# A weight load cut in two column halves, and the order of two steps' side work, in a fused attention and GELU kernel

## The chip, the cores and the metric

The kernel runs on one core of one Trainium2 chip. The metric is the time of the program on the device in microseconds (us): the median of 3 runs is 198.84 us (198.81 to 199.01).

## What is computed

A linear attention with decay, for 4 batches, 8 heads, 768 positions and 64 channels per head, and then a feed-forward pair of matrix products with a GELU (tanh form) between them. Cut to what matters:

```python
for b in range(nb):                       # blocks of 64 positions
    intra = einsum('bhic,bhjc->bhij', qb, kb) * Dmask     # scores, masked and decayed
    intra = einsum('bhij,bhjd->bhid', intra, vb)
    inter = einsum('bhid,bhde->bhie', qb * lam_pow, kv_state)
    out[:, :, sl] = intra + inter
    kv_state = lam_block * kv_state + einsum('bhsd,bhse->bhde', kb * rev_pow, vb)
x = out.transpose(0, 2, 1, 3).reshape(3072, 512)
h = x @ w_in                              # 512 x 2048
g = 0.5 * h * (1 + tanh(c * (h + 0.044715 * h ** 3)))
return g @ w_out                          # 2048 x 512
```

Inputs and the output are float32; the matrix products run on float16 copies.

## The kernel before

**Steps.** The attention is worked in 24 steps. A step is 256 positions of four of the eight heads (`half`) of one batch; two steps make a block of 256 rows of x. A step `s` passes through these pieces, each a small function:

- `load_step` issues three DMAs (q, k, v, 256 KB each, in rows of 512 bytes) on the queue of SyncE (SP).
- `prep` scales q by its decay and casts it (L282, VectorE, called DVE in the profile), casts k (L295, ScalarE, called ACT; at step 4 L293 on DVE), and scales v (L266, GpSimd, called POOL).
- `stage_t` transposes q and k for steps 0 to 7: eight 128x128 matmuls against the identity (L321, TensorE, called PE) into the PSUM tile Tps, and one copy to the tile qkT (L328 on ACT for steps 5 and 6, L330 on DVE for steps 4 and 7; steps 0 to 3 share it between the two). From step 8 on a transposing DMA does it (L303).
- `scores(n)` makes the scores S from qkT: 16 matmuls on 64x64 tiles (L350).
- `products(n, s)` makes step n's update of the state, K (L385), and step s's outputs, from the masked scores PT and v (L399) and from the state u and q (L408), all in two PSUM tiles named OK. With `evacuate` it ends with `x_out(s)`: ACT copies OK to xT, the x of the feed-forward part (two copies, L487).
- `causal(n)` multiplies S by the mask into PT: two operations on DVE (L360).
- `update(n, c, parts)` carries the state on: part "t" on DVE (L506, or L503 at a batch's start), part "u" on POOL (L513).

`R(n, s)` is a helper that calls `scores(n)`, `products(n, s)`, `causal(n)` and `update(n, 0)` in that order; `U(n)` is `update(n, 1)`. At step 5, the last of its batch in its half, `U` issues nothing.

**Weights.** `load_win(j, part)` loads the quarter j of w_in (512 of its 2048 columns, L94); the first two quarters come in two parts of 512 KB each (`part` chooses half of the 512 rows). `cast_win` makes the float16 copies: the second part of the first quarter is cast by ACT for columns 0 to 255 (two operations of 128 columns, L108) and by DVE for columns 256 to 511 (one operation, L110). The matmuls of the feed-forward part's first product read them (L838 for the first group of rows, L561 after that). SP's queue has, in this order: q, k, v of steps 0 to 2, q and k of step 3, the first part of quarter 0, v of step 3, the second part of quarter 0, the rest of w_in, w_out, and q, k, v of steps 4 to 8. A DMA is issued when its tile is free.

**Order.** `pin` keeps every instruction in the order in which it is written, on its engine. So the order is written out by hand, at the function's end. The feed-forward work (product one: Hps, then GELU; product two: O2ps, four matmuls to a piece, L576; later groups MX, MY and MW, L640, in which sums of weights, made on DVE at L133, stand in for some of the products) is kept in the list `filler`, and `fill(n)` issues the next n pieces of it between the attention's steps: this is what TensorE does while other engines prepare the next step. [...]

Around the change the order is: `products(3, None)`, `causal(3)`, the casts of the second part of quarter 0 (ACT and DVE), `update(3, 0)`, `fill(4)` (the first four pieces to read these casts), `products(None, 3)`; and, later, `R(5, 4)`, `stage_t(6)`, `U(5)`, `prep(7)`, a sum of weights on DVE, `fill(2)`, `R(6, 5)`, `U(6)`, `fill(1)`, `prep(8)`.

Of the kernel before, what the change touches and what calls it, by code (L numbers as in the profile page):

```python
# [15 lines left out]
def kernel(  # L16
# [10 lines left out]
    nc = tc.nc  # L27
    pin = tc.keep_in_program_order
# [59 lines left out]
    def load_win(j, part=None):  # L88
        if not part:
            wstage[("i", j)] = wst.tile([P, NC, 512], FP32, tag=f"w{j}", name=f"wi32_{j}")  # L90
        t = wstage[("i", j)]
        src = moe_w_in[:, j * 512 : (j + 1) * 512].rearrange("(c p) f -> p c f", p=P)
        cs = slice(0, NC) if part is None else slice(2 * part, 2 * part + 2)
        pin(nc.sync.dma_start(out=t[:, cs, :], in_=src[:, cs, :]))  # L94

    def load_wout(j):
        t = wst.tile([P, 4, DM], FP32, tag=f"w{(0, 2, 1, 3)[j]}", name=f"wo32_{j}")
# [147 lines left out]
    def prep(s):  # L245
        prep_qk(s)
        prep_v(s)
# [61 lines left out]
    def stage_t(s):  # L309
        if s >= FIRST_DMA_T:  # L310
            return
        tq, tk = a16[s][:2]
        if s < 4:
            Tps = [ps_M.tile([P, 2, 2, P], FP16, tag="M", name=f"Tps{i}") for i in range(2)]
        else:
            Tps = ps_M.tile([P, 2, 2, 2, P], FP16, tag="M", name="Tps")
        for i, t in enumerate((tq, tk)):
            to = Tps[i] if s < 4 else Tps[:, i]
            for hp in range(2):
                for j in range(2):  # L320
                    pin(nc.tensor.transpose(to[:, j, hp, :], t[:, j, 2 * hp : 2 * hp + 2, :],  # L321
                                            ident[:]))
        o = qkp.tile([P, 2, 2, 2, P], FP16, tag="qkT", name=f"qkT_{s}")
        if s < 4:
            pin(nc.scalar.activation(out=o[:, 0], in_=Tps[0][:], func=AF.Copy))
            pin(nc.vector.tensor_copy(out=o[:, 1], in_=Tps[1][:]))
        elif s in (5, 6, 8):
            pin(nc.scalar.activation(out=o[:], in_=Tps[:], func=AF.Copy))  # L328
        else:
            pin(nc.vector.tensor_copy(out=o[:], in_=Tps[:]))  # L330
        qkT[s] = o
# [7 lines left out]
    def half64(i):  # L339
        return slice(64 * i, 64 * i + 64)  # L340
# [3 lines left out]
    def scores(n):  # L344
        o = qkT[n]
        Sps = [ps_M.tile([P, 2, 2, P], FP32, tag="M", name=f"S{hl}") for hl in range(2)]
        for hp in range(2):
            for jk in range(2):
                for hl, c in TILES:
                    pin(nc.tensor.matmul(  # L350
                        Sps[hl][half64(c), hp, jk, :], o[half64(hl), 1, jk, hp, half64(c)],
                        o[half64(hl), 0, :, hp, half64(c)], start=True, stop=True,
                        skip_group_check=True))
        Ss[n] = Sps

    def causal(n):

        t = ptp.tile([P, 2, 2, 2, P], FP16, tag="PT", name=f"PT_{n}")
        for hl, Sps in enumerate(Ss.pop(n)):
            pin(nc.vector.tensor_tensor(  # L360
                t[:, hl].rearrange("p b c d -> p b (c d)"), Sps[:].rearrange("p b c d -> p b (c d)"),
                mask[:].unsqueeze(1).to_broadcast([P, 2, 2 * P]), ALU.mult))
        PTs[n] = t

    def products(n, s, banks=None, evacuate=True):


        OK, opened = banks or ([ps_M.tile([P, 512], FP32, tag="M", name=f"OK{c}")
                                for c in range(2)], set())

        def start(c, hl):
            if (c, hl) in opened:
                return False
            opened.add((c, hl))
            return True

        if n is not None:
            _, tk, tv = a16[n]
            last = (n // 2) % NSB == NSB - 1
            for jk in range(2):  # L380
                for hp in range(2):
                    for c, hl in TILES:
                        if c == 1 and last:
                            continue
                        pin(nc.tensor.matmul(  # L385
                            OK[c][half64(hl), 256 + hp * D : 256 + hp * D + D],
                            tk[half64(c), jk, 2 * hp + hl, :], tv[half64(c), jk, 2 * hp + hl, :],
                            start=start(c, hl), stop=(jk == 1), skip_group_check=True))
            Kps[n] = [t[:, 256:384] for t in OK]
        if s is None:  # L390
            return OK, opened
        sbg, half = divmod(s, 2)
        o = qkT.pop(s)
        PT = PTs.pop(s)
        _, _, tv = a16.pop(s)
        for hp in range(2):
            for jk in range(2):
                for c, hl in TILES:
                    pin(nc.tensor.matmul(  # L399
                        OK[c][half64(hl), hp * P : hp * P + P], tv[half64(c), jk, 2 * hp + hl, :],  # L400
                        PT[half64(c), hl, hp, jk, :], start=start(c, hl), stop=False,
                        skip_group_check=True))
        for c in range(2):
            if c == 0 and sbg % NSB == 0:
                continue
            u = us.pop((s, 0) if c else (s - 2, 1))
            for hp in range(2):
                pin(nc.tensor.matmul(OK[c][:, hp * P : hp * P + P], u[:, hp].rearrange("p l d -> p (l d)"),  # L408
                                     o[:, 0, :, hp, half64(c)], start=False, stop=True,
                                     skip_group_check=True))  # L410
        if evacuate:
            x_out(s, OK)
        return OK, opened
# [61 lines left out]
    def x_out(s, OK, second=None):  # L475
        sbg, half = divmod(s, 2)
        g, i = group_of[sbg]
        if g not in xT:
            xT[g] = xtp.tile([P, 2, len(groups[g]), 2, SB], FP16, tag="xT", name=f"xT_{g}")
        dst = xT[g][:, half, i]  # L480
        for c in range(2):
            d = dst[:, :, c * P : (c + 1) * P].rearrange("p hp (t j) -> p hp j t", j=2)
            o = OK[c][:, 0:256].rearrange("p (hp j t) -> p hp j t", hp=2, j=2)
            if c == 1 and second is not None:
                pin(second.tensor_copy(out=d, in_=o))
            else:
                pin(nc.scalar.activation(out=d, in_=o, func=AF.Copy))  # L487
# [3 lines left out]
    def update(s, c, parts="tu"):  # L491


        sbg, half = divmod(s, 2)
        sb = sbg % NSB
        if c == 1 and sb == NSB - 1:
            Kps.pop(s)
            return
        if "t" in parts:
            K = (Kps[s] if c == 0 else Kps.pop(s))[c].rearrange("p (hp d) -> p hp d", hp=2)  # L500
            t = ucp.tile([P, 2, D], FP32, tag=f"t{half}", name=f"t_{s}_{c}")
            if sb == 0 and c == 0:
                pin(nc.vector.tensor_copy(out=t[:], in_=K))  # L503
            else:
                for hp in range(2):
                    pin(nc.vector.scalar_tensor_tensor(  # L506
                        t[:, hp, :], state[half][:, hp, :],
                        lamu[:, 2 * half + hp : 2 * half + hp + 1], K[:, hp, :],
                        ALU.mult, ALU.add))
            state[half] = t  # L510
        if "u" in parts:
            u = ubp.tile([P, 2, 2, D], FP16, tag=f"u{half}", name=f"u_{s}_{c}")
            pin(nc.gpsimd.tensor_tensor(  # L513
                u[:], state[half][:].unsqueeze(2).to_broadcast([P, 2, 2, D]),
                lumask[:, 2 * half : 2 * half + 2, :].unsqueeze(3).to_broadcast([P, 2, 2, D]),
                ALU.mult))
            us[(s, c)] = u
# [388 lines left out]
    def fill(n):  # L906
        for _ in range(min(n, len(filler))):
            filler.pop(0)()

    def R(n, s, ahead=None, keep=False):  # L910

        if n is not None:
            scores(n)
        if ahead:
            ahead()
        products(n, s)
        if n is not None:
            causal(n)
        if s is not None and s % 2 == 1:
            g, i = group_of[s // 2]  # L920
            if i == len(groups[g]) - 1 and g > 0:
                queue_group(g)
        if n is not None and not keep:
            update(n, 0)

    def U(n):
        update(n, 1)
# [74 lines left out]
    U(4)  # L1002
    prep(6)
    fill(2)
    R(5, 4)
    stage_t(6)
    U(5)
    prep(7)
    sum_wout(1, 3, DVE)
    fill(2)  # L1010
    R(6, 5)
    U(6)
    fill(1)
    prep(8)
    fill(1)
    stage_t(7)
# [144 lines left out]
```

## Time and profile before

| | |
|---|---|
| median of 3 runs | 198.84 us |
| the profiled execution: time, span | 198.79 us, 197.0 us |
| PE busy | 191.2 us (97%) |
| DVE busy | 149.0 us (76%) |
| ACT busy | 121.1 us (61%) |
| POOL busy | 74.4 us (38%) |
| chain that ended last | PE 89%, SP's queue 4%, DMA 4% |
| granted TensorE clock | 1.00 throughout |
| read from HBM, written to it | 27.26 MB, 6.29 MB |

The profile is of one execution. Times in it count from the start of the span. A row of the timeline has the start in us, the duration in us, engine, line and operation, what is written and read, the shape, and how many instructions are merged; in brackets, how long the engine had been idle before it and what ended that. PE is TensorE's matmuls, PEld its weight loads; matmuls are pipelined and their ends are modelled, so the next one can start before the row's end. SPq is a DMA that SyncE's queue issues, at the time of issue; the data lands later. The page cuts the span in 40 slices of 4.9 us; a digit is the busy share of a slice in tenths. In a table of windows, each row has the window, its length, the busy time of PE, PEld, DVE, ACT and POOL with the number of instructions, the clock, DMA's share and GB/s.

Waits of PE over the whole execution, as the profile counts them, are few: 0.8 us for a DVE copy near 12 us, 0.8 us at the start, 0.5 us for POOL near 13 us, and 0.35 us at 18.24 us, for a cast of ACT.

### The profile page before, as it was taken

How to read it: one execution, taken by the hardware profiler on the slowest of the kernel's cores; microseconds unless marked ns; L12 is line 12 of the kernel's file. 1: busy time of each engine (PE TensorE's matmuls, PEld its weight loads, DVE VectorE, ACT ScalarE, POOL GpSimd, SP SyncE). 2: the span in 40 equal slices, each digit the busy share in tenths (PEclk: the TensorE clock that was granted, in tenths of full speed). 3: DMA queues.
4: the chain of work that ended last, by engine and by line, in shares of the span. 5: the costliest groups of instructions: out<-in, count | busy, mean ns of one | idle time of the engine just before them, and what ended most of it. 6: DMA issues, size and time to landing. Idle time of an engine off the chain costs nothing.

```text
span 197.0 us, 5913 instructions
## 1 busy us (share of the span) xinstructions
PE 191.2 (97%) x2431; PEld 140.1 (71%) x2431; DVE 149.0 (76%) x291; ACT 121.1 (61%) x249; POOL 74.4 (38%) x85
## 2 busy tenths in 40 slices
PE   8979999999999999999999999999999999999993
PEld 2556544446888888654688764578888888888882
DVE  4797722889999889859999927999656987487620
ACT  3663878357874685686845378844867746679221
POOL 6594213457554931169754517165002030002000
PEclk9999999999999999999999999999999999999999
DMA  5999999999999999999996998400211300020205
GB/s 167 292 324 384 387 383 386 300 285 297 259 220 248 257 333 231 213 238 288 226 294 132 274 310 202 92 7 0 53 67 42 107 6 2 0 110 29 77 19 198
DMA packets 62810, 38.13 MB, mean 194 GB/s; under 512 B 18624, under 2 KB 55744, under 8 KB 62784
## 3 DMA queue, kind: packets, MB, share of 16 engines
q1 hardware_dynamic: 62240, 37.50, 74.3%
q8 instruction: 19, 0.31, 0.7%
q10 hardware_dynamic: 544, 0.26, 0.5%
q14 instruction: 7, 0.06, 0.1%
HBM read 27.26 MB, written 6.29 MB: 170 GB/s over the span
## 4 chain that ended last, share of the span: by engine, by line
PE 89%; SPq 4%; DMA 4%; ACT 0%; issue 0%
PE Hps L561 25%; PE MX L640 18%; PE MY L640 9%; PE HX L739 7%; PE O2ps L576 7%; PE MW L640 4%; DMA wi<-in_moe_w_in_dram 4%; SPq L70 4%; PE HY L739 4%; PE S L350 3%; PE Hps L838 3%; PE HW L739 2%; PE OK L408 2%; PE O L461 1%; PE O L436 1%; PE OK L399 1%
## 5 line engine op out<-in xcount | busy, mean ns | idle before, releaser
L561 PE MATMUL Hps<-xT,w_in 128*128 128x512 f16 (+1 forms) x288 | 50.5, 332 | 0.0
L513 POOL TENSOR_TENSOR u<-t,lumask 128x256 f16<-128x256 f32 x40 | 30.9, 788 | 40.7 <-DVE t L506 27.0
L561 PEld LDWEIGHTS <-w_in 128*128 128x128 f16 x288 | 27.9, 98 | 19.1
L565 ACT ACTIVATE gT<-Hps 128x512 f16<-128x512 f32 x56 | 33.5, 598 | 11.6 <-PE Hps L561 11.1
L360 DVE TENSOR_TENSOR PT<-S,mask 128x512 f16<-128x512 f32 x48 | 30.3, 680 | 7.8 <-PE S L350 7.8
L266 POOL TENSOR_TENSOR v<-v,dv 128x512 f16<-128x512 f32 x24 | 28.7, 1197 | 15.2 <-DMA v<-in_v_dram 14.0
L640 PEld LDWEIGHTS <-gs 128*128 128x128 f16 x320 | 31.2, 98 | 3.6
L640 PEld LDWEIGHTS <-gT 128*128 128x128 f16 x240 | 23.3, 98 | 3.2 <-ACT gT L565 0.2
L640 PE MATMUL MX<-w_sum,gs 128*128 128x256 f16 x160 | 21.4, 273 | 0.0
L692 POOL TENSOR_TENSOR o<-u,q 128x512 f32<-128x512 f32 (+1 forms) x5 | 6.3, 1252 | 36.7 <-ACT u L657 36.7
L282 DVE TENSOR_TENSOR qk<-q,dq 128x512 f16<-128x512 f32 x23 | 19.1, 833 | 0.8 <-DMA q<-in_q_dram 0.7
L295 ACT ACTIVATE qk<-k 128x512 f16<-128x512 f32 x23 | 14.4, 625 | 7.4 <-DMA k<-in_k_dram 7.3
L610 DVE TENSOR_TENSOR gs<-gT 128x1024 f16<-128x1024 f16 (+1 forms) x24 | 16.9, 711 | 1.6 <-ACT gT L565 1.6
L576 PE MATMUL O2ps<-w_out,gT 128*128 128x512 f16 x64 | 14.6, 379 | 0.0
L487 ACT ACTIVATE xT<-OK 128x256 f16<-128x256 f32 x26 | 9.9, 452 | 7.0 <-PE OK L408 6.5
L739 PEld LDWEIGHTS <-ws 128*128 128x128 f16 x128 | 12.5, 98 | 1.6 <-issue 0.2
L487 ACT ACTIVATE xT<-O 128x256 f16<-128x256 f32 x22 | 8.0, 461 | 5.8 <-PE O L461 4.9
L657 ACT ACTIVATE u<-MX 128x256 f32<-128x256 f32 x18 | 6.9, 384 | 7.4 <-PE MX L640 7.3
L576 PEld LDWEIGHTS <-gT 128*128 128x128 f16 x64 | 6.1, 98 | 6.6
L350 PEld LDWEIGHTS <-qkT 64*64 64x64 f16 x384 | 6.0, 106 | 6.8 <-issue 3.6
L640 PE MATMUL MY<-w_out,gs 128*128 128x256 f16 x80 | 10.7, 273 | 0.0
L753 DVE COPY u<-HX 128x512 f32<-128x512 f32 x8 | 5.5, 688 | 6.8 <-ACT gT L757 4.3
(98 smaller groups left out, 318.4 us busy)
## 6 DMA issues: line engine op xcount, KB each, us to landing
q<-in_q_dram SPq DMA_DIRECT2D x24, 256.0 KB, 4.9
k<-in_k_dram SPq DMA_DIRECT2D x24, 256.0 KB, 5.0
v<-in_v_dram SPq DMA_DIRECT2D x23, 256.0 KB, 5.2
out_dram<-o SPq DMA_DIRECT2D x23, 256.0 KB, 4.3
wo<-in_moe_w_out_dram SPq DMA_DIRECT2D x4, 1024.0 KB, 9.4
wi<-in_moe_w_in_dram SPq DMA_DIRECT2D x4, 512.0 KB, 7.1
wi<-in_moe_w_in_dram SPq DMA_DIRECT2D x2, 1024.0 KB, 12.5
v<-in_v_dram ACTq DMA_DIRECT2D x1, 256.0 KB, 4.3
```

The lines of the kernel that those rows point to most:

```text
L266: pin(nc.gpsimd.tensor_tensor(wide(tv[:]), ld32[s][2][:], decay(dv, s), ALU.mult))
L282: pin(q_eng.tensor_tensor(wide(tq), q32[:], decay(dq, s), ALU.mult))
L295: pin(nc.scalar.activation(out=wide(tk), in_=k32[:], func=AF.Copy))
L360: pin(nc.vector.tensor_tensor(t[:, hl].rearrange("p b c d -> p b (c d)"), Sps[:].rearrange("p b c d -> p b (c d)"), mask[:].unsqueeze(1).t ...
L487: pin(nc.scalar.activation(out=d, in_=o, func=AF.Copy))
L513: pin(nc.gpsimd.tensor_tensor(u[:], state[half][:].unsqueeze(2).to_broadcast([P, 2, 2, D]), lumask[:, 2 * half : 2 * half + 2, :].unsqueez ...
L561: pin(nc.tensor.matmul(by_block(Hps[:, i, :]), w_in16[:, c, f * P : (f + 1) * P], x(c), start=(c == 0), stop=(c == NC - 1)))
L565: pin(nc.scalar.activation(out=dst, in_=Hps[:], func=AF.Gelu_apprx_tanh))
L576: pin(nc.tensor.matmul(O2[tau][0][:], gT[:, f % HF, f // HF, tau * P : (tau + 1) * P], w_out16[:, f, :], start=(n == 0), stop=(n == NF - 1)))
L610: pin(nc.vector.tensor_tensor(g_rows(m, i), g_rows(a, i), g_rows(b, i), op))
L640: pin(nc.tensor.matmul(dst, lhsT, rhs, start=(opens and i == 0), stop=(closes and i == HF - 1), skip_group_check=True))
L739: pin(nc.tensor.matmul(dst[:, i, :], w_in_block(a, slice(c, c + 1), slice(f * P, f * P + P))[:, 0], x_block(b, slice(c, c + 1))[:, 0], sta ...
```

## The change

Two edits. First, the second part of quarter 0 of w_in is loaded by two DMAs, for columns 0 to 255 and 256 to 511, one behind the other on the same queue, each 256 KB in rows of 1 KB instead of one DMA of 512 KB in rows of 2 KB. Second, in place of `R(5, 4)` its parts are written out in another order: after the products, part "t" of step 5's state comes first, then `stage_t(6)`, then the copies of step 4's outputs (`x_out`), then step 5's masks, then part "u". And one piece of feed-forward work moves from in front of `R(6, 5)` to behind `U(6)`.

```diff
@@ load_win
         cs = slice(0, NC) if part is None else slice(2 * part, 2 * part + 2)
-        pin(nc.sync.dma_start(out=t[:, cs, :], in_=src[:, cs, :]))
+        for fs in (slice(0, 256), slice(256, 512)) if (j, part) == (0, 1) else (slice(0, 512),):
+            pin(nc.sync.dma_start(out=t[:, cs, fs], in_=src[:, cs, fs]))
@@ the order at steps 5 and 6
     U(4)
     prep(6)
     fill(2)
-    R(5, 4)
+    scores(5)
+    out_4 = products(5, 4, evacuate=False)[0]
+    update(5, 0, "t")
     stage_t(6)
+    x_out(4, out_4)
+    causal(5)
+    update(5, 0, "u")
     U(5)
     prep(7)
     sum_wout(1, 3, DVE)
-    fill(2)
+    fill(1)
     R(6, 5)
     U(6)
-    fill(1)
+    fill(2)
     prep(8)
     fill(1)
     stage_t(7)
```

No operation is added or removed on TensorE, DVE, ACT or POOL.

## The prediction

> **What bounds the kernel now.** I read the page first: busy times, then the slices.
>
> ```profile
> PE 191.2 (97%) x2431; PEld 140.1 (71%) x2431; DVE 149.0 (76%) x291; ACT 121.1 (61%) x249; POOL 74.4 (38%) x85
> ...
> DMA  5999999999999999999996998400211300020205
> ```
>
> TensorE is the bound (97%), but DMA digits stand at 9 from 5 us to beyond 100 us: early on, a matmul can be late only because its input has landed late. So the change is worth what it does to PE's idle time, place by place. PE ends are modelled (a 128x128 transpose shows 219 ns, the next starts 56 ns later), so I looked for distances from start to start longer than columns / 2.4 ns. After the first 15 us three kinds are left: a regular 0.095 us at each change between 64-row and 128-row tiles; a wait near 18 us; a wait near 42 us. (Later there is one of 0.16 us at 137.4 us, and nothing else.) The timeline at 18 us:
>
> ```profile
> 17.57 0.32 PE L385 MATMUL OK<-v,qk 64*64 64x64 f16 x16
> 17.77 0.72 ACT L108 ACTIVATE w_in<-wi 128x256 f16<-128x256 f32 x2 [1.66 <-DMA wi<-in_moe_w_in_dram]
> 17.77 0.43 DVE L110 CAST w_in<-wi 128x512 f16<-128x512 f32 x1 [0.51 <-DMA wi<-in_moe_w_in_dram]
> 18.11 0.47 DVE L506 SCALAR_TENSOR_TENSOR t<-t,lamu,OK 128x64 f32<-128x64 f32 x2
> ...
> 18.24 1.13 PE L838 MATMUL Hps<-xT,w_in 128*128 128x256 f16 x8 [0.35 <-ACT w_in L108]
> ...
> 18.54 0.55 PEld L838 LDWEIGHTS <-w_in 128*128 128x128 f16 x6 [0.19 <-ACT w_in L108]
> 18.65 1.36 POOL L513 TENSOR_TENSOR u<-t,lumask 128x256 f16<-128x256 f32 x2 [1.14 <-DVE t L506]
> 19.12 1.18 DVE L110 CAST w_in<-wi 128x512 f16<-128x512 f32 x2 [0.55 <-DMA wi<-in_moe_w_in_dram]
> ```
>
> Here the second part of the first weights lands at 17.75 us, ACT casts two blocks, and PE waits: 0.35 us, then some 0.1 us more for the second block (0.19 us on the weight load). About 0.5 us is the most that this place can give. Then the timeline at steps 4 and 5:
>
> ```profile
> 37.73 0.92 DVE L282 TENSOR_TENSOR qk<-q,dq 128x512 f16<-128x512 f32 x1 [0.53 <-DMA q<-in_q_dram]
> ...
> 38.64 0.43 DVE L293 CAST qk<-k 128x512 f16<-128x512 f32 x1
> ...
> 38.92 0.61 PE L321 MATMUL Tps<-ident,qk 128*128 128x128 f16 x8
> ...
> 41.40 0.63 ACT L295 ACTIVATE qk<-k 128x512 f16<-128x512 f32 x1 [3.51 <-DMA k<-in_k_dram]
> ...
> 42.08 0.23 PEld L321 LDWEIGHTS <-qk 128*128 128x128 f16 x4 [0.20 <-ACT qk L295]
> ```
>
> The fifth transpose of step 4 starts at 38.92 + 4 x 0.056 = 39.14 us; the k that it reads is cast at 38.64 + 0.43 = 39.07 us, and the q before it came straight from its DMA. Some 0.03 us of play. At step 5 PE really waits 0.20 us for k, which ACT casts as soon as it has landed. **So at 42.09 us PE runs by the DMA stream, not by its own past.** The chain of waits hides this, since it follows modelled matmul ends. Last, step 6:
>
> ```profile
> 45.07 0.61 PE L321 MATMUL Tps<-ident,qk 128*128 128x128 f16 x8
> 45.16 0.77 ACT L487 ACTIVATE xT<-OK 128x256 f16<-128x256 f32 x2 [0.19 <-PE OK L408]
> 45.52 1.89 PE L576 MATMUL O2ps<-w_out,gT 128*128 128x512 f16 x8
> ...
> 45.78 1.02 ACT L328 ACTIVATE qkT<-Tps 128x1024 f16<-128x1024 f16 x1
> ...
> 47.34 0.42 PE L350 MATMUL S<-qkT 64*64 64x128 f16 x16
> ```
>
> The scores of step 6 (S) need the copy qkT, done at 46.80 us. PE doesn't wait: eight O2ps matmuls cover it until 47.25 us.
>
> **What the Trainium skill says.** "DMA: Bandwidth & Descriptors", section "Why small descriptors are slow (HBM only)": each packet carries a fixed overhead, so smaller rows move slower. The trace agrees (386 against 293 GB/s, below). "ScalarE: Activation LUTs", section "What ACT_TABLE_LOAD costs": an activation with immediates takes 186 ns + 0.833 ns per element: 1.04 us for 1024, and the trace has 1.02. "TensorEngine Tiling (Array Packing)", section "Key Properties": changing the tiling mode drains the array; the trace has 0.095 us per change, and the change adds none. "PSUM — Partial Sum Buffer", section "Engine vs sequencer instructions": ACT, DVE and POOL are strict queues, so what stands behind a waiting instruction waits too.
>
> **Part 1, the split load.** Removed: one DMA of 512 KB with 2 KB rows; added: two of 256 KB with 1 KB rows. No byte less, and every later load stands behind it in the same queue. The pace of rows, from windows with one row size each (weights at 21 to 34 us, q, k and v at 42.5 to 46.5 us; the last number is GB/s):
>
> ```profile
> 21.00:34.00 13.00, 13.00 (x66) 6.21 (x64) 4.87 (x11) 10.71 (x19) 2.75 (x3) 1.00 1.05 386
> 42.50:46.50 4.00, 4.00 (x65) 2.37 (x64) 3.34 (x9) 3.81 (x8) 2.77 (x4) 1.00 1.13 293
> ```
>
> Over 16 DMA engines a 2 KB row takes 16 x 2048 / 386 = 85 ns, a 512 B row 16 x 512 / 293 = 28 ns. A straight line gives 9 ns + 0.037 ns per byte, 47 ns for 1 KB (an estimate). Each engine carries 32 rows x 47 - 16 x 85 = 144 ns more, and one more completion of about the fixed 9 ns: **0.15 us later for everything behind it.** Bounds: nothing (if the rows' cost is hidden; a gain is excluded, since no load is shortened or moved ahead), and 0.43 us (if 1 KB rows were as slow per byte as 512 B rows: 64 x 28 - 16 x 85). SP issues one DMA more (0.46 to 0.77 us in its rows); the next weights are issued before 14 us, and their data has its turn near 17.8 us, so that costs nothing.
>
> At 18 us: the first half lands near 17.15 us, ACT's casts are ready when PE needs them, and 0.35 us goes. But DVE's cast now waits for the second half, near 17.9 us instead of 17.74, and queued behind it are the state (18.11 to 18.26 us) and, for POOL, u (18.65 to 18.80 us), which PE needs for its L408 matmuls at 19.65. With u ready near 19.5 us, and the next weights' cast (19.12 + 0.15 + 0.43 = 19.70 us, then 0.05 for the semaphore), PE's first 128x512 matmul comes at 19.75 instead of 19.89 us. 0.14 us of the gain is left, and the stop at step 4 (0.03 us of play, and q and k 0.15 us later) takes it. At step 5, k lands 0.15 us later, so PE resumes at 42.24 instead of 42.09 us. **Part 1: +0.15 us**, and its gain of 0.35 us is turned into a longer wait for k.
>
> **Part 2, steps 5 and 6.** The instruction lists of the two programs differ in three things only: DVE's state t of step 5 stands ahead of its two masks, ACT's copy qkT of step 6 ahead of the two xT copies, and four O2ps matmuls stand behind the scores and products of step 6. No DMA moves. Counted in the times of before (all of this shifts with k):
>
> - ACT: qkT waits for the eighth transpose[...] at 45.69 us with the semaphore, and starts some 0.08 us later, as an idle ACT does behind k at 41.32 to 41.40. That is 45.78 us, where it starts today. The xT copies ahead of it cost it nothing. It ends at 46.80 us as now.
> - PE: four O2ps matmuls instead of eight, 45.52 + 4 x 0.216 = 46.38 us, + 0.095 for the tile mode: PE asks for S at 46.47 us and gets qkT at 46.80 + 0.05 = 46.85 us. **+0.38 us of idle PE**, which the four matmuls covered. Bounds: 0.33 to 0.48 us from the granularity of these rows; nothing, if the copy starts earlier than I read.
> - The moved matmuls (0.86 us) now stand before Hps, where xT of step 5 was ready already; nothing there was waiting, so they hide nothing.
> - DVE: t runs at 45.16 to 45.62 us, the masks end at 46.83 instead of 45.89 us; the products need them at 47.20 us. POOL's u comes 0.6 us sooner, without use. xT of step 4 ends near 47.4 us, needed near 49.5; k of step 7 is cast 0.5 us later, needed at 50.4. The o copy and k of step 8 come some 0.3 us later, and with them SP's transposing DMA of step 8, landed at 55.15 us for scores at 58.55.
>
> After that PE has no wait that could give the time back. **Sum:** 198.79 us profiled (span 197.0, 1.8 around it) + 0.15 + 0.38 = 199.32; the median of the runs is 0.05 higher, so 198.84 + 0.53 = 199.37 us.
>
> **Rivals.** *k of step 5 doesn't land later* (its pace is set by something other than row cost): only part 2 counts, 198.84 + 0.38 = 199.22 us. For it: q, k and v already show dips of the rate; against it: digits of 9 throughout. *No stop at step 6*, the one that ends not slower: the copy qkT begins sooner once xT is out of its way. It decides from a start at 45.40 us, 0.38 us earlier, while the last transpose starts at 45.46; for it stands only that ACT's xT and qkT rows touch. It gives 198.99. *The front's gain survives*: v of step 3 was cast only at 16.47 us, so an uneven share of one DMA engine may delay all later landings; were that gone, both waits (0.5 + 0.2 us) would go: 198.84 - 0.7 + 0.38 = 198.52, and without the stop at step 6 198.14. Nothing in the change touches what precedes 16 us. *A further wait*: masks later than the products want them, or the transposing DMA missing its slot: 199.8. That the program isn't changed as told is excluded by the instruction lists.
>
> **Numbers.** Measurement tells about 0.2%, 0.4 us. Forecast 199.37: 0.63. Further wait 199.8: 0.05 (slower 0.68). k not later, 199.22: 0.10; no stop, 198.99: 0.09; gain survives but step 6 stops, 198.52: 0.03 (within 0.2%: 0.22). Both waits gone and no stop, 198.14: 0.10 (faster). The range, 198.9 to 199.7, holds the first, third and fourth.
>
> **What would show it.** Right: PE's L838 at 17.8 us without a wait on ACT; v, q and k loads from step 4 on landing 0.1 to 0.2 us later; PE's fifth transpose of step 5 waiting longer than 0.20 us; an idle 0.3 to 0.4 us of PE before S of step 6, released by ACT's qkT. Wrong: k of step 5 landing no later or earlier, or S of step 6 starting straight behind four O2ps matmuls.

## The result, and the profile after

| | before | after |
|---|---|---|
| median | 198.85 us (13 runs, 198.76 to 199.34) | 199.49 us (13 runs, 199.30 to 200.82) |
| ratio | | 1.0038, 95% interval 1.0021 to 1.0055 |

The change costs 0.64 us; 0.53 us had been forecast (199.37). The whole interval lies above 1, with its lower end at 0.21%; the prediction took 0.2% for the least that a measurement here can tell. Run again beside the experiments, the changed kernel took 199.44 us (11 runs) against 198.83: 1.0025, 1.0014 to 1.0037.

The first profile of the changed kernel (200.17 us) caught a stretch in which TensorE was granted a mean of only 0.58 of its clock, from 14.0 to 18.1 us; no other profile here has that. Two executions of the kernel before (199.46 and 199.66 us) have the same mean clock over the whole span, 0.991, so nothing ties it to the change, and the second profile, of an execution of 199.31 us, is read. Its page first, busy times and DMA's slices:

```profile
PE 191.7 (97%) x2431; PEld 140.1 (71%) x2431; DVE 148.9 (75%) x291; ACT 121.2 (61%) x249; POOL 73.7 (37%) x85
...
DMA  6999999999999999999996998400211300020205
```

The counts of instructions are those of before, and DMA's digits are too, but for the first slice. Nothing in these totals tells the faster kernel from the slower: the change is all in where things wait. The timeline at 18 us:

```profile
17.19 0.72 ACT L109 ACTIVATE w_in<-wi 128x256 f16<-128x256 f32 x2 [1.14 <-DMA wi<-in_moe_w_in_dram]
...
17.84 1.19 PE L839 MATMUL Hps<-xT,w_in 128*128 128x256 f16 x8
17.93 0.43 DVE L111 CAST w_in<-wi 128x512 f16<-128x512 f32 x1 [0.73 <-DMA wi<-in_moe_w_in_dram]
...
18.41 0.33 PEld L839 LDWEIGHTS <-w_in 128*128 128x128 f16 x4 [0.25 <-DVE w_in L111]
18.82 1.37 POOL L514 TENSOR_TENSOR u<-t,lumask 128x256 f16<-128x256 f32 x2 [1.30 <-DVE t L507]
...
19.77 0.33 PEld L839 LDWEIGHTS <-w_in 128*128 128x128 f16 x3 [0.17 <-DVE w_in L111]
```

ACT has its half at 17.19 instead of 17.77 us, PE starts without a wait at 17.84 instead of 18.24. But DVE's cast starts at 17.93 instead of 17.77 us, PE now waits for that one (0.25 us on the weight load), u starts at 18.82 instead of 18.65, and the first weights of the next group, where PE waits again, are taken at 19.77 us. The timeline at steps 4 and 5:

```profile
38.79 0.90 PE L322 MATMUL Tps<-ident,qk 128*128 128x128 f16 x8
38.80 0.43 DVE L294 CAST qk<-k 128x512 f16<-128x512 f32 x1 [0.18 <-DMA k<-in_k_dram]
39.28 0.23 PEld L322 LDWEIGHTS <-qk 128*128 128x128 f16 x4 [0.28 <-DVE qk L294]
...
41.49 0.63 ACT L296 ACTIVATE qk<-k 128x512 f16<-128x512 f32 x1 [3.43 <-DMA k<-in_k_dram]
...
41.81 0.77 PE L322 MATMUL Tps<-ident,qk 128*128 128x128 f16 x8
```

Matmuls one behind the other start 56 ns apart for 128 columns, 109 ns for 256 and 216 ns for 512 in the trace of the kernel before (53 ns for 128 more columns, 107 ns for 256 more: 2.4 columns per ns, as the prediction has it). PE comes to step 4 at 38.79, 0.13 us ahead of before, and loses that and more at its fifth transpose: k's cast, which DVE began straight behind q's before, now waits for its DMA and ends at 39.23 us. At step 5 PE would be through its fourth transpose at 41.81 + 4 x 0.056 = 42.03 us; it goes on at 42.18, when ACT's cast (41.49 + 0.63) is there, after 0.15 us of idle time. And step 6:

```profile
45.16 0.61 PE L322 MATMUL Tps<-ident,qk 128*128 128x128 f16 x8
...
45.61 1.03 PE L577 MATMUL O2ps<-w_out,gT 128*128 128x512 f16 x4
45.64 1.28 DVE L361 TENSOR_TENSOR PT<-S,mask 128x512 f16<-128x512 f32 x2
45.87 1.02 ACT L329 ACTIVATE qkT<-Tps 128x1024 f16<-128x1024 f16 x1 [0.67 <-PE Tps L322]
...
46.95 0.42 PE L351 MATMUL S<-qkT 64*64 64x128 f16 x16 [0.31 <-ACT qkT L329]
```

Four matmuls now stand between the transposes and S. From the first of them to S it takes 46.95 - 45.61 = 1.34 us; four matmuls and the change from 128-row to 64-row tiles take 4 x 0.216 + 0.095 = 0.96. PE is idle for 0.38 us (the bracket says 0.31, since the matmuls' ends are modelled), and ACT's copy ends it. Nothing overlaps here that didn't before: ACT, now free of the xT copies, still starts 0.26 us behind the first O2ps matmul (45.87 - 45.61; before 45.78 - 45.52). In these two profiles PE's last matmul of the program comes 0.47 us later than before: 0.09 us are there at step 5 (42.18 against 42.09), and 0.38 come at step 6.

### The profile page after: what moved, and what is told of

Read it like the earlier page. It is cut to its first block, busy times and chain, and to the rows that moved or that the text cites. A ratio compares the mean times of both kernels' runs of the same rounds, so it can differ in the third digit from the quotient of the medians.

```text
span 198.3 us, 5915 instructions
## 1 busy us (share of the span) xinstructions
PE 191.8 (97%) x2431; PEld 140.3 (71%) x2431; DVE 150.9 (76%) x291; ACT 121.0 (61%) x249; POOL 73.8 (37%) x85
## 4 chain that ended last, share of the span: by engine, by line
PE 90%; DMA 3%; POOL 2%; DVE 1%; SPq 1%; ACT 1%; issue 1%; ACTq 0%; POOLq 0%
PE Hps L562 24%; PE MX L641 17%; PE MY L641 8%; PE HX L740 7%; PE O2ps L577 7%; PE MW L641 4%; PE Hps L839 4%; PE HY L740 4%; PE S L351 4%; DMA v<-in_v_dram 3%; PE OK L409 2%; PE HW L740 2%; PE OK L400 2%; PE O L462 1%; PE Tps L322 1%; PE O L437 1%
## 5 line engine op out<-in xcount | busy, mean ns | idle before, releaser
L283 DVE TENSOR_TENSOR qk<-q,dq 128x512 f16<-128x512 f32 x23 | 20.1, 877 | 0.4 <-DMA q<-in_q_dram 0.4
L693 POOL TENSOR_TENSOR o<-u,q 128x512 f32<-128x512 f32 (+1 forms) x5 | 5.8, 1158 | 36.6 <-ACT u L658 36.6
L507 DVE SCALAR_TENSOR_TENSOR t<-t,lamu,OK 128x64 f32<-128x64 f32 x36 | 8.2, 274 | 3.4 <-PE OK L386 1.0
L351 PE MATMUL S<-qkT 64*64 64x128 f16 x384 | 9.3, 224 | 1.5 <-DVE qkT L327 1.2
```

Of the source, the lines that this page charges most:

```text
L283: pin(q_eng.tensor_tensor(wide(tq), q32[:], decay(dq, s), ALU.mult))
L351: pin(nc.tensor.matmul(Sps[hl][half64(c), hp, jk, :], o[half64(hl), 1, jk, hp, half64(c)], o[half64(hl), 0, :, hp, half64(c)], start=True, ...
```

## The experiments

Each kernel ran beside the kernel before, whose median in the three sets was 198.81, 198.83 and 198.83 us. Ratios are made over all the runs, so where single runs lie a microsecond or more above the rest they stand a little above the ratio of the medians.

### The two edits apart

**The split alone:**

```diff
-        pin(nc.sync.dma_start(out=t[:, cs, :], in_=src[:, cs, :]))
+        for fs in (slice(0, 256), slice(256, 512)) if (j, part) == (0, 1) else (slice(0, 512),):
+            pin(nc.sync.dma_start(out=t[:, cs, fs], in_=src[:, cs, fs]))
```

> Part 1 alone, the load in two halves. My theory: the wait at 18 us goes, but every later load lands some 0.15 us later and PE waits the longer for k of step 5; PE's second half of the transposes of step 5 starts at 42.2 us instead of 42.1, and the time is 0.15 us above before (199.0 us). Rival, the split's gain survives: 0.3 us below before. Rival, the whole loss of 0.6 us comes from the split: 199.5 us.

Measured: 198.97 us (13 runs), +0.16; ratio 1.0008 (0.9997 to 1.0018). The interval includes 1, so these runs alone don't prove a loss. The timeline at steps 4 and 5 shows where it would be:

```profile
39.09 0.43 DVE L294 CAST qk<-k 128x512 f16<-128x512 f32 x1 [0.18 <-DMA k<-in_k_dram]
...
39.57 0.40 PE L322 MATMUL Tps<-ident,qk 128*128 128x128 f16 x4 [0.21 <-DVE qk L294]
```

The split's price is paid at the first transposes that follow the loads closely, those of step 4: the fifth starts at 39.57 us, where it could have started at 38.96 + 4 x 0.056 = 39.19, so PE stands idle for 0.38 us. At step 5 a stop of only 0.08 us is left, and PE goes on at 42.40 us, where 42.2 had been expected.

**The order alone** (both edits of the second part, the load in one piece):

> Part 2 alone, both the new order at step 5 and the moved O2ps piece. My theory: PE waits 0.38 us for qkT of step 6, k of step 5 lands as before, and the time is 0.38 us above before (199.2 us). Rival, part 2 costs nothing by itself and hurts only behind a later k: 198.85 us.

Measured: 199.31 us (13 runs), +0.50; ratio 1.0023 (1.0015 to 1.0031). S of step 6 waits as in the full change, 1.34 - 0.96 = 0.38 us by the distance of starts:

```profile
45.55 1.03 PE L576 MATMUL O2ps<-w_out,gT 128*128 128x512 f16 x4
45.81 1.02 ACT L328 ACTIVATE qkT<-Tps 128x1024 f16<-128x1024 f16 x1 [0.66 <-PE Tps L321]
...
46.89 0.42 PE L350 MATMUL S<-qkT 64*64 64x128 f16 x16 [0.31 <-ACT qkT L328]
```

The two parts add up to 0.16 + 0.50 = 0.66 us; the change measured 0.64 and 0.61.

**The order, but with the feed-forward pieces where they were.** Only `R(5, 4)` is written out in the new order:

```diff
-    R(5, 4)
+    scores(5)
+    out_4 = products(5, 4, evacuate=False)[0]
+    update(5, 0, "t")
     stage_t(6)
+    x_out(4, out_4)
+    causal(5)
+    update(5, 0, "u")
```

> Only the new order of state, copy, xT and masks at step 5; all eight O2ps matmuls stay ahead of the scores of step 6. My theory: the copy qkT starts when the last transpose is done, as before (0.2 us behind it), and PE never waits for it: no change, 198.85 us. Rival, the new order itself costs PE (masks of step 5 0.9 us later, or xT later): 0.2 us or more above before, with a wait on DVE or ACT behind the scores of step 6.

Measured: 198.89 us (22 runs), +0.08; ratio 1.0012 (1.0000 to 1.0023). Timeline at step 6, the O2ps matmuls and S:

```profile
45.46 1.89 PE L576 MATMUL O2ps<-w_out,gT 128*128 128x512 f16 x8
...
47.28 0.42 PE L350 MATMUL S<-qkT 64*64 64x128 f16 x16
```

Eight matmuls and the change of tiles take 8 x 0.216 + 0.095 = 1.82 us, and S starts 1.82 us behind the first of them: no wait, with the copy qkT ahead of xT or behind it.

**The feed-forward piece alone**, moved behind `U(6)`, with `R(5, 4)` as it was:

```diff
-    fill(2)
+    fill(1)
     R(6, 5)
     U(6)
-    fill(1)
+    fill(2)
```

> Only the O2ps piece moved behind the scores of step 6; the order at step 5 as before. My theory: the same 0.38 us of idle PE before the scores of step 6 as with the new order, because the copy qkT starts no sooner with it: 199.2 us. Rival, the new order does bring the copy forward, and without it the wait is longer than 0.38 us (0.5 us or more).

Measured: 199.16 us (21 runs), +0.35; ratio 1.0017 (1.0011 to 1.0024). Timeline at step 6:

```profile
44.97 0.77 ACT L487 ACTIVATE xT<-OK 128x256 f16<-128x256 f32 x2
...
45.32 1.03 PE L576 MATMUL O2ps<-w_out,gT 128*128 128x512 f16 x4
45.58 1.02 ACT L328 ACTIVATE qkT<-Tps 128x1024 f16<-128x1024 f16 x1
...
46.66 0.42 PE L350 MATMUL S<-qkT 64*64 64x128 f16 x16 [0.31 <-ACT qkT L328]
```

Here the xT copies stand ahead of qkT on ACT, and the copy still starts 0.26 us behind the first O2ps matmul, as it does where it stands ahead of them: it waits for the transposes, not for ACT. S waits the same 0.38 us. So this one move is the larger part of the change's cost, and the copy's place at the front of ACT's queue does nothing against it.

### The cover taken away, and given back

**No O2ps piece at all ahead of S of step 6** (the changed kernel with `fill(3)` behind `U(6)`, and none before `R(6, 5)`):

```diff
-    fill(1)
     R(6, 5)
     U(6)
-    fill(2)
+    fill(3)
```

> The changed kernel with the other O2ps piece moved behind the scores of step 6 too, so that none stands between the transposes and the scores of step 6. My theory: the wait is what is left of the copy's 1.02 us and its two handovers, so each piece of 0.86 us moved away lengthens it by 0.86 us: 1.24 us of idle PE before the scores of step 6 instead of 0.38, 200.3 us. Rival, the loss isn't this wait but the later place of the pieces: less than 0.5 us more than the change.

Measured: 200.26 us (4 runs), ratio 1.0078 (1.0062 to 1.0094). That is 0.82 us above the changed kernel, for one piece of four matmuls of 0.216 us (0.86 us) taken out of the stretch.

```profile
46.99 0.42 PE L351 MATMUL S<-qkT 64*64 64x128 f16 x16 [1.17 <-ACT qkT L329]
```

S itself starts at 46.99 instead of 46.95 us: its time is set by ACT's copy, whatever stands ahead of it. Once the spare time is used up, what is taken from in front of it is lost in full: 0.82 us by the medians, 0.87 on TensorE (table below).

**The changed kernel with its second piece back** (the split and the new order, `fill(2)` and `fill(1)` as before):

> The changed kernel with the O2ps piece put back ahead of the scores of step 6. My theory: the 0.38 us go, the later loads stay: 0.15 us above before (199.0 us), no wait before the scores of step 6. Rival, the new order at step 5 makes up for the later loads: as before or faster (198.8 us or less).

Measured: 199.04 us (22 runs), ratio 1.0019 (1.0000 to 1.0038): 0.40 us below the changed kernel. In its profile S of step 6 starts 1.82 us behind the first O2ps matmul, without a wait, where the changed kernel waits 0.38 us. The profiled execution (199.92 us) is not a typical one: one transposing DMA came late at 88.45 us and stopped PE for 0.98 us (by the distance of starts), which no other profile shows; up to there it agrees with the others.

### The loads earlier: is it they that bound PE at steps 4 and 5?

**Half of the last w_out load left out.** These kernels leave out half of the last 1 MB load of w_out and cast the other half twice, so that all loads behind it come sooner; the products of those rows use the weights of the others, with the same instructions.

```diff
+        n = 2 if j == 3 else 4
-        pin(nc.sync.dma_start(out=t[:], in_=moe_w_out[j * 512 : (j + 1) * 512, :].rearrange(
-            "(c p) e -> p c e", p=P)))
+        pin(nc.sync.dma_start(out=t[:, 0:n], in_=moe_w_out[j * 512 : (j + 1) * 512, :].rearrange(
+            "(c p) e -> p c e", p=P)[:, 0:n]))
...
-            src = t[:, 2 * i : 2 * i + 2, :]
+            src = t[:, 0:2, :] if j == 3 else t[:, 2 * i : 2 * i + 2, :]
```

> The kernel before with half of the last 1 MB load of w_out left out (the second half of those weights is cast from the first half), so that 0.5 MB less stands ahead of q, k and v of steps 4 and 5. My theory: they land 1.3 us earlier, PE no longer waits for k of step 5, and the 0.2 us of that wait are gained: 198.65 us. Rival, the wait there is not the DMA's: no change, 198.8 us, with a wait left at step 5.

> The same with the load split in two halves as in the change (and half of the last load of w_out left out). My theory: with loads no longer the bound at steps 4 and 5, what the split saves at 18 us survives: 0.1 to 0.15 us faster than the short kernel without the split (198.5 us), and PE has no wait at steps 4 and 5. Rival, the later landing costs here too: 0.15 us slower than without the split (198.8 us).

Both missed: 199.66 us (7 runs; 1.0034, 1.0019 to 1.0049) without the split and 199.49 us (22 runs; 1.0021, 1.0005 to 1.0037) with it. The loads did come sooner, by 1.0 to 1.3 us: POOL has v of step 4 at 38.56 and 38.30 us instead of 39.57, ACT has k of step 5 at 40.28 and 40.06 instead of 41.40. What came in their place, in the timeline of the one without the split:

```profile
38.56 1.58 POOL L267 TENSOR_TENSOR v<-v,dv 128x512 f16<-128x512 f32 x1 [1.06 <-DMA v<-in_v_dram]
...
39.17 1.26 DVE L294 CAST qk<-k 128x512 f16<-128x512 f32 x1
...
40.48 0.40 PE L322 MATMUL Tps<-ident,qk 128*128 128x128 f16 x4 [0.58 <-DVE qk L294]
```

v is there while k's cast is still in DVE's queue, so POOL's scaling begins first and the cast takes 1.26 us instead of 0.43 (1.28 us in the other kernel), and PE waits for it: 0.74 us by the distance of starts (0.58 in the bracket). In the kernel before, POOL begins that scaling half a microsecond after the cast's end (38.64 + 0.43 = 39.07 us); the late loads kept the two apart:

```profile
39.57 1.04 POOL L266 TENSOR_TENSOR v<-v,dv 128x512 f16<-128x512 f32 x1 [1.47 <-DMA v<-in_v_dram]
```

The Trainium skill has a mechanism that fits, in "SBUF — State Buffer", section "Who interferes with whom": DVE and GpSimd share a pair of ports; where a DVE instruction runs in a mode that takes this pair too, which a cast can do, whichever of the two issues first holds the pair for its whole instruction, and the other blocks. The trace agrees in time: both casts end 0.28 to 0.29 us after POOL's row, though rows on POOL are rough. In which mode the cast ran no run shows. The clash doesn't account for all of the loss: counted from the landing of v of step 3, PE's fifth transpose of step 5 comes 0.57 us (without the split) and 0.45 us (with it) later than before, and the medians lie 0.83 and 0.66 us above. Of the second kernel's 22 runs three lie at 198.25 to 198.41 us and all others at 199.27 or above; the three stand near the 198.5 expected, but whether the clash was absent in them no profile shows.

**The same, with k of step 4 cast by ACT**, out of POOL's way:

```diff
-        if s == 4:
+        if s < 0:
```

> The short kernel again (half of the last load of w_out left out, its weights cast from the first half), with k of step 4 cast on ACT, so that this cast no longer runs on DVE beside POOL's scaling of v, which took 1.28 us instead of 0.43. My theory: now no wait of PE is left at steps 4 and 5, and 0.2 us are gained on before: 198.65 us. Rival, some other engine holds steps 4 and 5: 198.8 us or more.

> The same with the load split in two halves (half of the last load of w_out left out too). My theory: where loads don't bound steps 4 and 5, the split's 0.1 to 0.15 us at 18 us survive: 0.1 to 0.15 us below the same kernel without the split. Rival, the later landing costs here too: 0.15 us above it.

Measured: 198.79 us (13 runs; 1.0001, 0.9992 to 1.0010) without the split, 199.05 us (21 runs; 1.0019, 1.0005 to 1.0033) with it. In the first, timeline at steps 4 and 5:

```profile
37.31 0.63 ACT L296 ACTIVATE qk<-k 128x512 f16<-128x512 f32 x1 [0.73 <-DMA k<-in_k_dram]
...
41.63 0.62 PE L322 MATMUL Tps<-ident,qk 128*128 128x128 f16 x8
```

The eight transposes run in one piece: the fifth starts 0.24 us behind the first, at 41.87 instead of 42.09 us. PE's last matmul of the program comes 0.23 us sooner, as expected; but in this execution it took 3.09 us instead of 2.87 from the end of ACT's last copy to the end of the span, so that the span is as long as before; the median lies 0.04 us below. That the loads bound PE at step 5 by some 0.2 us is shown on TensorE; what it is worth at the end of the program is not.

The second missed: without the waits at steps 4 and 5 the split should have gained some 0.1 us, and its median lies 0.26 us above the first. In the profile the gain is there, if one counts from the landing of v of step 3 (table below), but that landing was itself 0.25 us later than in the first, and the end took 3.42 us. Other profiles give no sign that the split brings these about: with it the landing was followed by POOL's start at 16.33 to 16.52 us and the end took 2.82 to 2.94 us, without it the two are 16.31 to 17.06 us and 2.86 to 3.09 us. Why the median is higher stays open.

**k of step 5 cast by DVE instead of ACT** (kernel before; DVE's sum of weights ahead of it moved behind `prep(6)`):

```diff
-        if s == 4:
+        if s in (4, 5):
...
-    sum_wout(1, 2, DVE)
     fill(2)
     R(4, None)
     stage_t(5)
     U(4)
     prep(6)
+    sum_wout(1, 2, DVE)
```

> The kernel before with k of step 5 cast on DVE (0.43 us) instead of ACT (0.63 us), and the sum of weights that held DVE then moved 3 us later. My theory: PE's wait of 0.2 us for k of step 5 goes, and nothing else becomes late: 198.65 us. Rival, another input of steps 4 or 5 takes its place, or DVE's later work does: 198.8 us or more.

Measured: 199.14 us (19 runs), +0.31; ratio 1.0013 (1.0006 to 1.0020): the rival's side. The wait for k is gone, PE goes on at 42.05 us although v of step 3 had landed 0.15 us later in this execution. But DVE, with the sum now behind `prep(6)`, runs late from there on: its last gs (L610) starts at 62.13 us instead of 61.73, and PE is stopped for it, for 0.20 us by the distance of starts.

```profile
63.44 0.33 PEld L640 LDWEIGHTS <-gs 128*128 128x128 f16 x4 [0.31 <-DVE gs L610]
```

## Why the prediction was right, step by step

The profiled executions differ at the start by how v of step 3 landed, so I measure from there. The first column is the start of POOL's scaling of that v; then, from it, the start of DVE's cast of the second part of quarter 0, PE's first 128x512 matmul of the feed-forward part, and PE's fifth transpose of step 5; the last is from that transpose to PE's last matmul. All in us, from the rows of each trace.

| kernel | v of step 3 | to the cast | to the first 128x512 | to k of step 5 | from there to PE's last |
|---|---|---|---|---|---|
| before | 16.47 | 1.30 | 3.42 | 25.62 | 151.36 |
| order alone | 16.44 | 1.33 | 3.45 | 25.68 | 151.74 |
| order, pieces kept | 16.45 | 1.29 | 3.41 | 25.58 | 151.36 |
| piece alone | 16.31 | 1.32 | 3.44 | 25.58 | 151.75 |
| split alone | 16.50 | 1.45 | 3.30 | 25.90 | 151.36 |
| split, order, pieces kept | 16.49 | 1.46 | 3.30 | 25.73 | 152.32 (late DMA) |
| after | 16.48 | 1.45 | 3.29 | 25.70 | 151.74 |
| after, no cover | 16.52 | 1.45 | 3.30 | 25.70 | 152.61 |
| half load left out, k of step 4 on ACT | 16.44 | 1.29 | 3.42 | 25.43 | 151.35 |
| the same, split | 16.69 | 1.45 | 3.29 | 25.28 | 151.35 |

- **The split's price in the queue: 0.15 us forecast, 0.13 to 0.15 measured.** In every kernel with one DMA the second part is there 1.29 to 1.33 us after v of step 3, in every kernel with two 1.45 or 1.46. The straight line between 512 B and 2 KB rows was good enough for 1 KB: it gave 47 ns, and the DMA records of the changed kernel's trace have 49 ns for these rows (median of 512; 88 ns for 2 KB, 31 ns for 512 B). They show one thing more. All but 28 of the 512 rows start before 16.0 us, and the last ones follow each other 48 ns apart until 17.34 us, at the pace of a single engine. So the load lands when what looks like one late engine is done; something like the uneven share of the prediction's third rival is there, and the split doesn't remove it.
- **The gain at the front: PE's first 128x512 matmul at 19.75 us forecast, 19.77 measured.** From v's landing 3.29 to 3.30 us in place of 3.41 to 3.45: 0.13 us, where 0.14 had been forecast. The wait of 0.35 us did go, and came back as waits for DVE's cast, as the queue on DVE required.
- **The gain lost again by step 5: +0.15 us forecast, +0.14 measured** in the mean of the four kernels with the split and all loads (25.76) against the four without (25.62), with a spread of 0.2 us among the former; the changed kernel's own profile has +0.08. The landing of k of step 5 says the same: 24.81 to 24.91 us behind v of step 3 without the split, 24.93 to 25.13 with it, 0.14 us in the mean. By the medians of the runs the split costs 0.16 us alone, 0.11 (0.61 - 0.50) on top of the new order, and 0.13 (0.21 - 0.08) where the piece stays; the intervals of these runs are as wide as that, so it is the traces that carry this step. Here it was right in sum and wrong in place. I had let the stop at step 4 take only the 0.14 us and put the loss in the wait for k of step 5, to be longer than 0.20 us. The changed kernel shows 0.15 us there, and step 4's fifth transpose has the rest: its play of 0.03 us became a stop of 0.27 us (39.28 - 38.79 - 4 x 0.056). The prediction's own numbers gave that: k's cast 0.15 us later, 39.07 + 0.15, and 0.05 to the matmul put the fifth transpose at 39.27 us, so PE had to leave step 4 some 0.13 us late and could not wait much longer than before at step 5. The two are stops on the same stream of loads, and what is lost at the first isn't lost at the second; the sum held because k's cast still bounds PE at step 5, with a stop of 0.08 to 0.20 us in all four kernels. How far one profile can be trusted here: the order alone, without the split, has a stop of 0.10 us at step 4 as well.
- **The idle time before S of step 6: 0.38 us forecast, 0.38 measured** in the three kernels where only four matmuls cover the copy, and nothing where eight do. The last column says it without any bracket: 151.36 us with the piece, 151.74 without, and 152.61 without either. The 1.25 us of that last step is 0.38 plus 0.87, the length of one more piece. That the copy "starts where it starts today" held too: 0.26 us behind the first O2ps matmul in all orders. The rival without a stop at step 6 (198.99) is out.
- **Nothing given back later.** The same column is the same to 0.01 us in kernels of one cover: DVE's later masks, ACT's later xT copies and the transposing DMA of step 8 cost PE nothing. Those steps, costed at nothing, held.
- **What the sum missed**: 0.64 and 0.61 us against 0.53. By medians the new order of `R(5, 4)` costs 0.08 us without the moved piece, and 0.15 with it (0.50 - 0.35); the profile of the order with the pieces kept shows no wait for that (PE's last matmul comes 176.94 us behind v of step 3, before 176.98), and the interval of its runs starts at 1.0000. Whether it is a cost is open.

The rival with the surviving gain is not excluded by the experiments as cleanly as I wanted. In the profiles the gain of 0.13 us does reach step 5 once the loads are early enough (25.28 against 25.43 us), and is lost when they aren't; the medians of those two kernels say the contrary, for reasons that I can't show. In the kernel as changed, the loads are not early enough, and that is what the forecast needed. Of the other rivals, the one in which k of step 5 lands no later (199.22) fails on that landing, 0.14 us later in the mean, and on the medians of the change, and the further wait (199.8) is not in the changed kernel's second profile; in its first, the one with the low clock, PE waited 0.3 us for DVE near 64 us.

## What to carry to other kernels

A wait that isn't there may be covered, and the cover has a length that can be counted: before moving work from in front of an instruction, work out when the instruction would be reached without that work, and compare with the time at which its input is there (here 46.47 against 46.85 us); one piece of 0.86 us was moved where only 0.86 - 0.38 = 0.48 us could be spared. Taking an operation to the front of its engine's queue gains nothing if it is its input that comes last. And where loads bound a later stage, a split that lets one engine start sooner is paid by all that is queued behind it.

## What the hardware showed beside

- Some work on DVE took two to three times as long beside work on POOL: a cast of 128x512 1.26 and 1.28 us instead of 0.43, and sums of 128x1024 float16 1.52 instead of 0.68 us (all in the kernels with half a load left out). Loads that come sooner can bring the two together.
- From the last copy on ACT to the end of the span it took 2.82 us (after) to 3.42 us from one profile to another, with the same final instructions: of the same size as the effects studied here. A gain of 0.2 us on TensorE can be lost there in a single execution.
- A modelled end hides short waits: the 0.38 us at step 6 reads 0.31 in its bracket, the 0.74 us at step 4 with half a load left out 0.58, and the 0.15 us at step 5 of the changed kernel has no bracket at all. Distances from start to start show all three.
